# Block sums of batch 0's q and k: VectorE reductions in place of matmuls with a constant, with a new order of all steps

## The chip, the core and the metric

The kernel runs on one core of one Trainium2 chip. The core has five engines with a queue each: TensorE (PE) multiplies matrices into PSUM, VectorE (DVE) and ScalarE (ACT) work on PSUM and SBUF, GpSimd (POOL) works on SBUF alone, SyncE (SP) issues DMA transfers; GpSimd and ScalarE can issue them too. An engine takes the instructions of its queue in order and waits on semaphores for the others. The metric is the device time of one execution in microseconds (us); lower is better.

## The reference

The computation is an attention layer with two branches and a feed-forward layer behind it. Batch is 8, heads 8, sequence 576, head size 64.

```python
q_d = q.reshape(B, H, Sd, 4, D).mean(axis=3)      # the same for k_d and v_d
out_d = sm_attn(q_d, k_d, v_d)                    # full softmax attention over 144 means
out_up = np.repeat(out_d, 4, axis=2)
mask = np.abs(pos[:, None] - pos[None, :]) < 4
scores = np.where(mask, scale * q @ k.T, -1e9)    # scale = 1/8
out_local = softmax(scores) @ v
x = (out_up + out_local)                          # to (4608 tokens, 512)
h = x @ w_in                                      # 512 x 2048
g = np.where(h > 0, h, np.exp(np.minimum(h, 0)) - 1)
return g @ w_out                                  # 2048 x 512
```

The means of four consecutive rows of q and k are what the change is about: they are the "coarse" queries and keys.

## The kernel before

The work goes by batch and, within a batch, by pairs of heads (j = 0 to 3): two heads of 64 fill the 128 partitions. For each pair q and k are loaded with the tokens on the partitions, turned so that the head's dimension is on the partitions, and copied from PSUM to SBUF. The scores of near keys and of coarse keys go to PSUM, ScalarE takes the exponential, TensorE sums the denominators with indicator matrices, VectorE takes reciprocals, TensorE spreads these over the partitions, and a product of values and exponentials is scaled by them (the normalisation). Near and coarse parts are added into tiles of 512 tokens (`xt`). The feed-forward layer takes these tiles t = 0 to 8: 16 products with `WI` per tile (`h`), the activation by ScalarE and VectorE (`he`, `hg`), and for tiles 0 to 5 the products with `WO` (`y`), a copy (`yc`) and a store (`ys`). Tiles 6 to 8 go by a scheme of seven products of half-size blocks (`sm`, `p`, `pk`, `pf`, `ps`, with weight differences `wd`).

Batch 0 has code of its own, since everything waits for it. Its pairs 1 to 3 come by loads that cast to 16 bits on the way (`lc`, on GpSimd's queue, `load_cast`, L371); pair 0 comes in 32 bits on SP's queue (`lx`) and is cast by ScalarE and VectorE (`cx`, L405). `transposes` (L486, step `T`) turns q into the PSUM tile `tq` and k into `tk`; both come from the two-buffer tag `misc` (`one`, L302). For batch 0 it then forms the block sums on TensorE as well: twelve matmuls per tensor (six for pair 0) with the constant `R` write them into columns 736 to 1023 of the same PSUM tile (L507 to L523). Four evictions follow for each pair: `eq` and `ek` copy the turned q and k to `QT` and `KT` (L528, L535), `sq` and `sk` copy the sums to `qd` and `kd` (`first_sums`, L1140). `first_scores` (L1152, step `s.j.g`, for half g of the sequence) needs all four. `R` holds 0.25 at the right places (L163), so `qd` and `kd` are means.

For batches 1 to 7 the sums already come from the turned tensors: `sums` (L547) reduces on VectorE (`"k"`, `"Q"`) or in two additions on GpSimd (`"q"`).

The order of all work is written out by hand in the string `ORDER` (L41). Each word is a step, such as `eq.0.2` for the copy of q of batch 0 and pair 2; `at` (L1241) binds it to a function, and a word with `'` takes the other variant, mostly another engine (`on_dve`, `on_act`). Each engine's queue is its steps in the order of this string. Buffers with more than one copy take the copy that `SLOTS` (L231) lists. `Z` steps and the `fills` (L1273) are matmuls on zeros between the real ones.

The steps that the prediction follows are: `T`, `eq`, `ek`, `sq`, `sk`, `s`, `x` (exponentials), `fD`, `fdr`, `fP`, `fpc`, `fO`, `fN`, `fna` of batch 0 (denominators, reciprocals, spread, its copy, outputs, normalisation, addition); and for batch 1 `m` (mask, L666), `D` and `dr` (denominators L678, reciprocals L699), `P` (spread, L759), among the feed-forward steps `h`, `he`, `hg` of tile 0.

Of the kernel before, what the change touches and what calls it, by code (L numbers as in the profile page):

```python
# [41 lines left out]
cI empties cN lc.0.2.k lc.0.2.q cR lc.0.1.k lc.0.3.k lc.0.1.q lx.0.0.k zeros edges Z.1 T.0.2.(0,2) eq.0.2'  # L42
ek.0.2' sq.2.q' cx.0.0.k sk.2.k' s.2.1.2 T.0.1.(0,0) Z.0 s.2.0.2 cVR lv.0.3 cIND cv.0.3 lc.0.3.q lv.0.1
lx.0.0.q close lc.1.0.q eq.0.1' sq.1.q' ek.0.1' sk.1.k' cx.0.0.q T.0.0.(1,0) s.1.0.0 eq.0.0' sq.0.q' ek.0.0
sk.0.k' x.2.0 lc.1.2.q lc.1.1.q T.0.3.(0,0) lv.0.0 lv.0.2 wi.0 wi.2 x.1.0 wi.1 cv.0.0 lc.1.0.k s.0.0.1 cFOUR
eq.0.3' sk.3.k' ek.0.3' sq.3.q' wi.3 cSEL cv.0.2' cv.0.1' fV.3 s.3.0.1 x.0.0 fD.0.0 fdr.0 x.2.1 x.3.0 s.0.1.1
fV.1 fvc.1' x.0.1 cIND2 cVR2 cMASK s.3.1.0 lv.1.0 x.3.1 fD.1.0 Z.2 s.1.1.0 lv.1.1 lx.2.1.q fdr.1 x.1.1 fvc.3
fP.0.0 fV.0 fvc.0' fO.0.1 fV.2 fpc.0 fN.0 fvc.2 fD.2.0 fdr.2 fP.1.1 fD.3.0 fpc.1 fna.0.0 fO.1.4 fN.1 fna.1.0'
lx.2.1.k H.0 H.1 fP.2.0 lx.2.3.q lx.2.0.q fdr.3 fpc.2 fO.2.0 fN.2 H.2 fP.3.0 H.3 lc.1.3.q lc.1.3.k lc.1.1.k
h.0.0 h.0.1 he.0.0 he.0.1' fO.3.2 lc.1.2.k cv.1.0 fpc.3' fN.3 fna.3.0 lv.1.2 T.1.0 h.0.7 h.0.5 T.1.3 ek.1.0  # L50
eq.1.0 fna.2.0 sq.1.0 wo.0 he.0.5 hg.0.1' sk.1.0 lv.1.3 lx.2.2.k hg.0.0 hg.0.5 eq.1.3 ek.1.3 T.1.1 eq.1.1
h.0.6 ek.1.1' lx.2.0.k sk.1.1 he.0.6' he.0.7 hg.0.7 hg.0.6' sq.1.1 sq.1.3 cv.1.1 fna.2.1 cv.1.2 h.0.8 T.1.2
he.0.8 eq.1.2 ek.1.2 h.0.9 sk.1.3 sk.1.2 sq.1.2' hg.0.8 lv.2.0 s.1.1 sd.1.1 h.0.15 x.1.1.0 he.0.15 x.1.1.1
m.1.1 Z.4 h.0.10 Z.3 he.0.10 hg.0.10 s.1.3 sd.1.3 x.1.3.0 x.1.3.1 hg.0.15 h.0.2 s.1.2 sd.1.2 x.1.2.0 he.0.2'
he.0.9 x.1.2.1 wo.1 cv.1.3 cx.2.0.q wo.2 cx.2.0.k cv.2.0 cx.2.1.q cx.2.1.k lv.2.1 m.1.2 m.1.3 hg.0.9 s.1.0
sd.1.0 h.0.11 h.0.12 hg.0.2' x.1.0.0 lx.2.2.q m.1.0 V.1 x.1.0.1 he.0.11 h.0.3 he.0.3 vc.1 D.1 fna.3.1' dr.1
P.1.3 h.0.4 P.1.1 hg.0.11 pc.1.1' pc.1.3 hg.0.3 P.1.2 y.0.0 he.0.4' pc.1.2 on.1.1 of.1.1 T.2.0 y.0.4 wo.3
lv.2.2 n.1.1 on.1.3 of.1.3 ek.2.0 eq.2.0 n.1.3 hg.0.4' cv.2.1 y.0.5 y.0.1 P.1.0 on.1.2 of.1.2 pc.1.0 he.0.12'
a.1.1.2 a.1.1.1' cx.2.2.q cx.2.2.k a.1.3.2' n.1.2 a.1.2.1 lv.2.3 lx.2.3.k lx.3.0.k cv.2.2 cx.2.3.q cx.2.3.k
cv.2.3' cx.3.0.k y.0.6 h.0.14 y.0.2 on.1.0 of.1.0 sk.2.0 a.1.3.1' hg.0.12' sq.2.0 n.1.0 a.1.0.1' y.0.7 T.2.1  # L60
eq.2.1 sq.2.1 y.0.3 yc.0.0 he.0.14 ek.2.1 yc.0.1' T.2.2 ek.2.2' hg.0.14 sk.2.2 h.1.0 h.0.13 he.1.0 eq.2.2
he.0.13' hg.1.0 sk.2.1 hg.0.13' T.2.3 h.1.1 lx.3.2.q lv.3.0 lx.3.1.k lx.3.1.q lx.3.0.q lv.3.1 lx.3.2.k s.2.0
sd.2.0 eq.2.3 a.1.2.2 sq.2.3 y.0.12 h.1.5 he.1.1' hg.1.1' ek.2.3 he.1.5' x.2.0.0 hg.1.5' y.0.8 h.1.7 he.1.7'
s.2.1 sd.2.1 x.2.0.1 x.2.1.0 x.2.1.1 m.2.0 sk.2.3 hg.1.7' sq.2.2' y.0.13 y.0.14 h.1.3 y.0.9 s.2.2 sd.2.2
he.1.3 fl.3.0 ys.0.1 ys.0.0 lv.3.2 lx.3.3.k hg.1.3 cx.3.0.q cv.3.0 T.3.0 cx.3.1.k cx.3.1.q cv.3.1 cx.3.2.k
# [1360 lines left out]
```

## Time and profile before

| what | value |
|---|---|
| timed runs | 346.63, 347.79, 340.81 us (median 346.63) |
| the profiled execution's own time | 340.41 us |
| its span, first to last instruction | 338.6 us |
| mean granted TensorE clock | 0.99 |
| DMA | 50.09 MB, mean 148 GB/s |

The page gives the busy time of each engine over the span, the span in 40 slices of 8.5 us, and the groups of instructions. In the views, "x12" counts instructions, the arrow is "out<-in", and a bracket holds the idle time of the engine ahead of an instruction with what ended it. TensorE's durations are modelled with their drain, so that neighbours overlap; start-to-start distances say how long a group holds the engine. Stage views have columns of busy us and counts per engine, then the granted clock, the DMA share and GB/s. Group views give count, busy us, mean ns of one, and the idle time before them.

### The profile page before, as it was taken

To read this page: it belongs to the slowest core of one execution; us is meant where nothing else is said; L and a number is where in the kernel's file an instruction comes from. 1 tells how busy PE (TensorE), PEld (TensorE's weight loads), DVE (VectorE), ACT (ScalarE), POOL (GpSimd) and SP (SyncE) were. 2 spreads that over 40 slices of the span, in tenths; PEclk is the share of its full clock that TensorE was granted. 3 is DMA by queue.
4 is the path that set the end of the run, shared out by engine and by line. 5 is a ranking of instruction groups with operands and counts; after the bars stand their busy time and mean duration, and the time that the engine had idled before them with its cause. 6 is when DMAs were issued, how large, how long until landed. Compare 5 with 4: busy or idle time off the path is not lost.

```text
span 338.6 us, 10715 instructions
## 1 busy us (share of the span) xinstructions
PE 326.5 (96%) x4378; PEld 195.1 (58%) x4378; DVE 246.0 (73%) x481; ACT 215.2 (64%) x375; POOL 176.3 (52%) x283
## 2 busy tenths in 40 slices
PE   7999987999999999999999999999999999999996
PEld 2666875564554545554545454545445566766785
DVE  1455986697878777777778868777885879697663
ACT  2084886368788785655678748665766578666520
POOL 4374746498186446553263347578301793550380
PEclk9999997899999999999999999999999999999999
DMA  8999999999999989979999999776015000030043
GB/s 171 224 173 208 247 221 223 210 202 163 183 198 156 190 207 197 199 163 161 200 201 203 173 200 164 174 160 113 2 37 151 5 0 0 2 149 9 0 157 124
DMA packets 111314, 50.09 MB, mean 148 GB/s; under 512 B 95697, under 2 KB 105761, under 8 KB 111265
## 3 DMA queue, kind: packets, MB, share of 16 engines
q1 hardware_dynamic: 106961, 43.04, 66.5%
q0 software_dynamic: 4064, 6.26, 10.6%
q8 instruction: 34, 0.56, 0.7%
q10 hardware_dynamic: 240, 0.11, 0.1%
q14 instruction: 15, 0.12, 0.1%
HBM read 41.97 MB, written 9.55 MB: 152 GB/s over the span
## 4 chain that ended last, share of the span: by engine, by line
PE 75%; DVE 9%; DMA 6%; ACT 4%; issue 3%; SPq 2%; POOL 0%; DVEq 0%; ACTq 0%; POOLq 0%
PE hp L904 28%; PE op L945 21%; PE y L1017 6%; PE xz L1017 5%; DMA q<-in_q_dram 4%; DMA out_dram<-os 3%; PE hp L880 2%; PE lg L784 2%; PE tqk L502 2%; DVE gt L935 1%; PE sc L632 1%; DVE e L934 1%; DVE ke L550 1%; ACT r L925 1%; PE den L692 1%
## 5 line engine op out<-in xcount | busy, mean ns | idle before, releaser
L904 PE MATMUL hp<-xt,WI 128*128 128x512 f16 x512 | 128.6, 380 | 1.3 <-DVE gt L930 0.7
L945 PE MATMUL op<-WO,gt 128*128 128x512 f16 x384 | 96.4, 383 | 0.1
L904 PEld LDWEIGHTS <-WI 128*128 128x128 f16 x512 | 55.7, 114 | 44.4 <-issue 1.7
L930 DVE SCALAR_TENSOR_TENSOR gt<-e,hp 128x512 f16<-128x512 f16 x78 | 53.0, 683 | 30.6 <-ACT e L926 30.3
L925 ACT ACTIVATE r<-hp 128x512 f32<-128x512 f32 x78 | 46.7, 599 | 38.3 <-PE hp L904 30.5
L945 PEld LDWEIGHTS <-gt 128*128 128x128 f16 x384 | 35.8, 98 | 40.5 <-issue 1.4
L915 ACT ACTIVATE e<-hp 128x512 f16<-128x512 f32 x66 | 39.3, 597 | 25.0 <-PE hp L904 18.8
L926 ACT ACTIVATE e<-r 128x512 f16<-128x512 f32 x78 | 49.2, 631 | 2.5
L935 DVE SCALAR_TENSOR_TENSOR gt<-hp,e 128x512 f16<-128x512 f32 x66 | 45.7, 692 | 2.6
L868 POOL TENSOR_TENSOR xt<-ln 128x192 f16<-128x192 f16 (+7 forms) x36 | 25.0, 706 | 33.8 <-DVE ln L857 30.3
L655 ACT ACTIVATE pex<-sc 128x580 f16<-128x580 f32 (+1 forms) x56 | 31.1, 591 | 4.0 <-PE sc L645 3.9
L934 DVE TENSOR_SCALAR e<-e 128x512 f16<-128x512 f16 x66 | 24.2, 366 | 12.5 <-ACT e L915 12.1
L476 POOL CAST v<-v 128x640 f16<-128x640 f32 (+1 forms) x19 | 14.4, 759 | 25.1 <-DMA v<-in_v_dram 21.9
L414 POOL CAST k<-k 96x768 f16<-96x768 f32 x24 | 20.3, 846 | 11.1 <-DMA k<-in_k_dram 11.1
L414 POOL CAST q<-q 96x768 f16<-96x768 f32 x24 | 19.7, 821 | 6.9 <-DMA q<-in_q_dram 6.8
L568 POOL TENSOR_TENSOR t<-qt 128x288 f32<-128x288 f16 x22 | 14.7, 668 | 16.2 <-ACT qt L532 11.9
L1017 PEld LDWEIGHTS <-gt 128*128 128x128 f16 x192 | 18.8, 98 | 5.6
L550 DVE TENSOR_REDUCE ke<-kt 128x145 f16<-128x580 f16 x28 | 21.0, 751 | 1.2 <-DMA kt<-k 1.1
L857 DVE TENSOR_TENSOR ln<-lg,rcb 128x580 f16<-128x580 f32 x28 | 21.0, 751 | 0.0
L995 POOL TENSOR_TENSOR s<-s,gt 128x512 f16<-128x512 f16 x8 | 9.8, 1224 | 19.3 <-DVE s L995 19.2
L880 PE MATMUL hp<-xt,WI 128*128 128x256 f16 x128 | 17.2, 283 | 1.3 <-DVE gt L935 1.2
L995 POOL TENSOR_TENSOR s<-gt 128x512 f16<-128x512 f16 x6 | 6.9, 1152 | 20.5 <-DVE gt L935 19.3
(148 smaller groups left out, 479.7 us busy)
## 6 DMA issues: line engine op xcount, KB each, us to landing
v<-in_v_dram SPq DMA_DIRECT2D x111, 80.0 KB, 4.2
k<-in_k_dram SPq DMA_DIRECT2D x25, 288.0 KB, 5.6
q<-in_q_dram SPq DMA_DIRECT2D x25, 288.0 KB, 6.5
out_dram<-os SPq DMA_DIRECT2D x24, 256.0 KB, 3.7
rcb<-rd SPq DMA_DIRECT2D x10, 364.0 KB, 5.6
out_dram<-ou SPq DMA_DIRECT2D x11, 256.0 KB, 2.2
WI<-in_moe_w_in_dram POOLq DMA_DIRECT2D x4, 512.0 KB, 9.5
WO<-in_moe_w_out_dram POOLq DMA_DIRECT2D x4, 512.0 KB, 7.4
```

The source lines that it names most:

```text
L414: nc.gpsimd.tensor_copy(out=x[:], in_=src)
L655: nc.scalar.activation(out=s["p"][:, :, a : a + n], in_=g2(sc, a, n), func=AF.Exp, scale=SCALE / 16 if a else SCALE,)
L868: (eng or nc.gpsimd).tensor_tensor(out=xt(t)[:, j, t0 - TBLK * t : t1 - TBLK * t], in0=ln[:, a:z], in1=_rep4(ln[:, ga : ga + (z - a) // 4] ...
L904: nc.tensor.matmul(hp, w_in(dc, fc), xts[t][:, dc, :], start=(dc == 0), stop=(dc == DMC - 1),)
L915: nc.scalar.activation(out=e, in_=hp, func=AF.Exp)
L925: nc.scalar.activation(out=r, in_=hp, func=AF.Relu, scale=-1.0)
L926: nc.scalar.activation(out=e, in_=r, func=AF.Exp, scale=-1.0)
L930: nc.vector.scalar_tensor_tensor(out=to, in0=e, scalar=-1.0, op0=AB.add, in1=hp, op1=AB.max)
L934: nc.vector.tensor_scalar(out=e, in0=e, scalar1=1.0, scalar2=-1.0, op0=AB.min, op1=AB.add)
L935: nc.vector.scalar_tensor_tensor(out=to, in0=hp, scalar=0.0, op0=AB.max, in1=e, op1=AB.add)
L945: nc.tensor.matmul(op_[:], gts[t][:, fc, 128 * tt : 128 * tt + 128], WO[:, fc, :], start=(fc == 0), stop=(fc == FCN - 1),)
L1017: nc.tensor.matmul(to, w, x, start=(k == 0 and n in (1, 2)), stop=(k == FH - 1), skip_group_check=n > 2,)
```

## The change

`transposes` no longer forms sums, the constant `R` and its load `cR` go, and `first_sums` reduces the copies `QT` and `KT` on VectorE. `sums(0, j, "Q")` is the reduction over four neighbours that later batches use; q's sums are then multiplied by 1/16 in place (a quarter for each of the two means), k's stay plain sums. `sq` and `sk` of batch 0 thus have no variant on ScalarE any more and come after `eq` and `ek` of their pair.

```diff
@@ transposes
-        if b == 0:
-            for t in (s["tq"], s["tk"]):
-                x = xs.pop(0)
-                for c in range(TPP):
-                    sums_of_4 = C["R"][:, SD * (c // 2) : SD * (c // 2) + SD]
-                    if j == 0:
-                        nc.tensor.matmul(
-                            t[:, 736:1024].bitcast(FP32), x[:, c, :, :].rearrange("p e d -> p (e d)"),
-                            sums_of_4, start=(c == 0), stop=(c == TPP - 1),
-                        )
-                        continue
...
@@ first_sums
-    def first_sums(j, x, copy=None):
-        s, copy = st[(0, j)], copy or act
+    def first_sums(j, x):
         if x == "q":
...
-            copy(out=s["qd"], in_=s["tq"][:, 736:1024].bitcast(FP32))
+            sums(0, j, "Q")
+            qd = st[(0, j)]["qd"]
+            nc.vector.tensor_scalar(out=qd, in0=qd, scalar1=0.0625, scalar2=None, op0=AB.mult)
             return
-        copy(
+        nc.vector.tensor_reduce(
             out=coarse_keys(0, j),
-            in_=s["tk"][:, 736:1024].bitcast(FP32).rearrange("p (c u) -> p c u", u=CG),
+            in_=KT[j][:, KO : KO + S].rearrange("p (c u f) -> p c u f", f=4, u=CG),
+            axis=AX.X, op=AB.add,
         )
```

`ORDER` and `SLOTS` are replaced as a whole: the same steps, without `cR`, in another order, many in another variant. The first lines of the order, before and after:

```diff
-cI empties cN lc.0.2.k lc.0.2.q cR lc.0.1.k lc.0.3.k lc.0.1.q lx.0.0.k zeros edges Z.1 T.0.2.(0,2) eq.0.2'
-ek.0.2' sq.2.q' cx.0.0.k sk.2.k' s.2.1.2 T.0.1.(0,0) Z.0 s.2.0.2 cVR lv.0.3 cIND cv.0.3 lc.0.3.q lv.0.1
+lc.0.2.q lx.0.0.q cVR lx.0.0.k lc.0.2.k empties zeros cI T.0.2.(0,2) ek.0.2 eq.0.2 sq.2.q sk.2.k edges
+lc.0.1.k Z.3 lc.0.1.q T.0.1.(0,0) cN cIND cVR2 lv.0.1 lc.0.3.k lc.0.3.q s.2.1.2 close ek.0.1 cx.0.0.k eq.0.1
...
```

Around batch 1's denominators (`D.1`), before and after:

```diff
-sd.1.0 h.0.11 h.0.12 hg.0.2' x.1.0.0 lx.2.2.q m.1.0 V.1 x.1.0.1 he.0.11 h.0.3 he.0.3 vc.1 D.1 fna.3.1' dr.1
-P.1.3 h.0.4 P.1.1 hg.0.11 pc.1.1' pc.1.3 hg.0.3 P.1.2 y.0.0 he.0.4' pc.1.2 on.1.1 of.1.1 T.2.0 y.0.4 wo.3
+hg.0.10 m.1.1 hg.0.9 s.1.2 sd.1.2 x.1.2.0 he.0.8' x.1.2.1 m.1.2 hg.0.8' h.0.4 Z.4 h.0.3 he.0.3 D.1 h.0.11 dr.1
+P.1.1 P.1.3 he.0.4 hg.0.4 pc.1.3' hg.0.3 pc.1.1 cv.1.3 V.1 h.0.12 vc.1 he.0.11 hg.0.11 on.1.3 on.1.1 of.1.3
...
```

Counted over the whole order: of batch 0's eight copies `eq` and `ek`, two run on VectorE (seven before); the four block-sum casts `fvc` all run on VectorE (two before); 73 of 144 activations take the form `he`/`hg` with one ScalarE pass and two VectorE passes (66 before); 16 of 32 casts of v run on ScalarE (13 before); one pair more of batches 3 to 7 is turned by TensorE instead of by a DMA (25 steps `T` without the mark, 24 before).

More of the change, by code (lines that the diff above doesn't have):

```diff
@@ L231 @@
 SLOTS = {
-    "end.hx": "0110101010101010",
-    "end.y": "010101",
+    "end.hx": "0101010101101101",
+    "end.y": "011010",
     "late.hp": (
-        "011010100010101010101001010100101010101010101010101010101101010101010101010101010101010101"
+        "010101100100101010101001010101010101010101101010101010101010101010101010101010101010010101"
         "010101010101010101010101010100101"
     ),
-    "lo.k32": "0120012012012010210210201",
-    "lo.q32": "0120010220121001201210210",
+    "lo.k32": "0120120210201201202102120",
@@ L259 @@
+    "sb.p": "0123456789ab42065317a9b842063517b98a",
+    "sb.qd": "01230123103213023102130231032130",
     "sb.rcb": "01010101",
-    "sb.v16": "01234567132057643120756403217456",
+    "sb.v16": "01234567103275640132756402314756",
     "sb.vdb": "0101010",
     "sb.xt": "012012012",
-    "tu.k16": "01230132013201320132012310321032",
-    "tu.pex": "0101010101010101010101",
-    "tu.q16": "01230102320132013201230130213031",
+    "tu.k16": "01230132103210321023012310231023",
+    "tu.pex": "0101010101010101010",
@@ L266 @@
+    "tu.q16": "01230132013201320132013210231031",
 }
@@ L505, in transposes @@
                 )
-        if b == 0:
-            for t in (s["tq"], s["tk"]):
-                x = xs.pop(0)
-                for c in range(TPP):
-                    sums_of_4 = C["R"][:, SD * (c // 2) : SD * (c // 2) + SD]
-                    if j == 0:
-                        nc.tensor.matmul(
-                            t[:, 736:1024].bitcast(FP32), x[:, c, :, :].rearrange("p e d -> p (e d)"),
-                            sums_of_4, start=(c == 0), stop=(c == TPP - 1),
-                        )
-                        continue
-                    for e in range(2):
-                        nc.tensor.matmul(
-                            t[64 * e : 64 * e + 64, 736:1024].bitcast(FP32),
-                            by_head(x)[:, e, D * c : D * c + D], sums_of_4,
-                            start=(c == 0), stop=(c == TPP - 1),
-                        )
     def in_order(t, to):
@@ L1283 @@
             at("lc", load_cast, 1, j, x)
-            at("sq" if x == "q" else "sk", first_sums, j, x, other=on_dve(first_sums))
+            at("sq" if x == "q" else "sk", first_sums, j, x)
         at("T", transposes, 0, j, fills["T"][j])
```

230 lines of the change are left out of this document (113 added, 117 removed).

## The prediction

> **What bounds the kernel now.** I read four views, in this order: the page's head and its 40 slices, the busy time by stage, the first 20 us in order of time, and the waits of TensorE.
>
> ```profile
> span 338.6 us, 10715 instructions
> PE 326.5 (96%) x4378; PEld 195.1 (58%) x4378; DVE 246.0 (73%) x481; ACT 215.2 (64%) x375; POOL 176.3 (52%) x283
> PEclk9999997899999999999999999999999999999999
> ```
> ```profile
> core 0: us, PE busy (x) PEld busy (x) DVE busy (x) ACT busy (x) POOL busy (x), PEclk, DMA share, GB/s
> 10.00:30.00 20.00, 18.18 (x419) 13.01 (x414) 11.02 (x27) 10.97 (x16) 8.57 (x14) 1.00 1.11 200
> 30.00:60.00 30.00, 26.95 (x526) 21.24 (x524) 23.84 (x47) 20.84 (x37) 19.90 (x37) 0.93 1.18 225
> 60.00:320.00 260.00, 258.46 (x3254) 144.33 (x3254) 201.01 (x371) 178.57 (x314) 133.52 (x216) 1.00 0.73 135
> 320.00:338.60 18.60, 15.28 (x137) 13.14 (x134) 8.71 (x17) 2.99 (x7) 9.63 (x9) 1.00 0.35 128
> ```
>
> TensorE is the bound: from 60 to 320 us it idles 260 − 258.46 = 1.5 us. Whatever ends sooner ahead of 60 us therefore moves the whole rest forward, one for one. The edit lies between 8 and 21 us, in the stage where TensorE is busy too (18.18 of 20 us), but in short pieces that hang on evictions; VectorE has 9 us free there. Between 30 and 60 us VectorE, ScalarE and TensorE limit each other, and the clock row dips: that is the one place where TensorE loses speed.
>
> ```profile
> 8.61 0.45 PE L497 MATMUL tq<-ID,q 96*64 96x96 f16 x12 [0.23 <-DMA q<-in_q_dram]
> 8.83 0.82 POOL L476 CAST v<-v 112x768 f16<-112x768 f32 x1 [4.19 <-DMA v<-in_v_dram]
> 9.60 1.25 POOL L373 DMA_DIRECT2D q<-in_q_dram  x2
> 9.81 0.54 PE L519 MATMUL tq<-R,q 96*64 96x144 f16 x12
> 10.19 0.54 PE L519 MATMUL tk<-R,k 96*64 96x144 f16 x12
> 10.40 0.76 DVE L532 COPY qt<-tq 128x576 f16<-128x576 f16 x1 [8.14 <-PE tq L519]
> 11.07 0.75 DVE L539 COPY kt<-tk 128x576 f16<-128x576 f16 x1
> 12.22 0.30 DVE L1147 CAST kd<-tk 128x144 f16<-128x144 f32 x1
> 12.57 0.29 PE L611 MATMUL sc<-qd,kd 64*112 64x72 f16 x4 [0.34 <-DVE kd L1147]
> 12.79 0.45 PE L497 MATMUL tq<-ID,q 96*64 96x96 f16 x12
> 17.05 0.54 PE L513 MATMUL tk<-R,k 96*128 96x144 f16 x6
> 18.37 0.45 PE L497 MATMUL tq<-ID,q 96*64 96x96 f16 x12 [0.16 <-DVE qd L1145]
> 31.38 0.91 DVE L835 TENSOR_TENSOR ln<-lg,rcb 128x720 f16<-128x720 f32 x1 [1.44 <-PE lg L823]
> 35.78 0.91 DVE L835 TENSOR_TENSOR ln<-lg,rcb 128x720 f16<-128x720 f32 x1 [0.53 <-PE lg L823]
> ```
>
> Here the reader sees one pair: transposes, sums on TensorE, four evictions on VectorE one behind the other, then the score. The next pair's transposes (12.79) come only when both PSUM buffers are read out.
>
> **The change, part by part.**
>
> *Sums off TensorE.* The rows at 9.81 and 10.19 start 0.38 us apart: twelve of these matmuls hold TensorE for 0.38 us. There are 36 + 36 + 6 + 6 = 84 in eight groups (the six at 17.05 are full-width and take as long), so 8 × 0.38 = 3.0 us of issue go.
>
> ```profile
> L519 PE MATMUL tq<-R,q 96*64 96x144 f16 x36 | 1.7, 226 | 0.0
> L513 PE MATMUL tk<-R,k 96*128 96x144 f16 x6 | 0.5, 226 | 0.0
> L1145 DVE CAST qd<-tq 128x144 f16<-128x144 f32 x4 | 1.2, 297 | 0.0
> L562 DVE TENSOR_REDUCE qd<-qt 128x144 f16<-128x576 f16 x1 | 0.7, 743 | 0.0
> L934 DVE TENSOR_SCALAR e<-e 128x512 f16<-128x512 f16 x9 | 3.4, 383 | 0.8 <-ACT e L915 0.8
> L388 DVE MEMSET q<- 1x1 f32 x3 | 0.2, 59 | 0.0
> L539 ACT COPY kt<-tqk 128x576 f16<-128x576 f16 x3 | 1.9, 643 | 0.0
> ```
>
> *Sums onto VectorE.* Eight reductions of 0.74 (the qd row is the very same shape) are 5.9 us; eight casts of 0.30 go, −2.4. Four multiplications of 128x144 in place have no row: at least 0.06 (a one-element memset), at most 0.38 (the 128x512 multiplication). I take 0.15, nearer the small end since 144 is a quarter of 512: 0.6 in all, bounds 0.2 to 1.5. Net +4.1 us of VectorE. A sentence on a page: the Trainium skill (VectorE: DVE Perf Modes, "The perf-mode tier table") gives a reduction one element per cycle and a 16-bit tensor_scalar up to four, which would put my multiplication at its lower end and change the sum by 0.3 us of VectorE at most.
>
> *Copies moved to ScalarE.* Before, seven of the eight first copies of tq and tk are VectorE's; after, two are. Five × 0.75 = −3.8 on VectorE, +5 × 0.64 = 3.2 on ScalarE. Two casts of v leave ScalarE for GpSimd, and the block-sum casts of v go to VectorE. VectorE ends within about 1 us of its load in this stage, ScalarE within 1 to 2 us. Both are about half idle from 10 to 30 us, so I cost the load itself at nothing; were that cover gone, it would cost up to the 4.1 us.
>
> *The chain of one pair.* What is not hidden is order: a sum now waits for its copy. For pair 2: transposes end at 9.98 in both, ScalarE's two copies end 1.15 later (0.5 apart and 0.64), and 0.7 + 0.1 + 0.7 of VectorE make 12.7, where 12.53 stood before. The first score is 0.15 us late. But the PSUM buffers are read out at 11.1, not 12.5, and the new order puts pair 1's transposes ahead of that score, so pair 1 starts 1.2 to 1.5 us sooner. The last score of each pair then waits for its k reduction, about 0.7 us behind the copy, under other pairs' transposes and scores. Following both orders pair by pair to the normalisation that feeds the first expert matmuls (31.38), I get 30.4: −1.0 us. Ends: −3.0, if all TensorE issue that goes was on the path, and +1.5, if two reductions in a row (1.5 us) hold the scores. I take −1.0, because the path goes through evictions more often than through TensorE.
>
> *Queues.* On GpSimd six loads of q and k are now issued one behind the other; before, the cast of v at 8.83, which waited 4.19 us for its data, stood ahead of pair 3's q load at 9.60. So pair 3 can be turned ahead of 18.37; that is in the walk. SP sends pair 0's q and k first and the mask constant behind them, about 1.5 us later than before and still about 8 us ahead of the first score. The constant's own load on ScalarE's queue goes: nothing, since ScalarE first waits for data anyway.
>
> *30 to 56 us, reordered.*
>
> ```profile
> PE den L692 <- DVE pex L670: 0.9, 1, 0.9
> PE rb L763 <- DVE rc L702: 0.8, 1, 0.8
> PE hp L880 <- DVE gt L935: 1.2, 3, 0.6
> ACT r L925 <- DMA out_dram<-os: 6.3, 3, 4.4
> ```
> ```profile
> 49.00:52.40 3.40, 3.17 (x54) 2.89 (x54) 2.56 (x8) 3.37 (x8) 2.33 (x5) 1.00 1.09 215
> 52.40:55.80 3.40, 1.66 (x69) 1.36 (x68) 2.76 (x5) 1.66 (x4) 1.24 (x3) 0.99 1.14 226
> 55.80:59.20 3.40, 3.40 (x26) 2.08 (x26) 1.15 (x3) 2.30 (x4) 3.03 (x7) 0.50 1.09 227
> 59.20:62.40 3.20, 3.20 (x44) 1.83 (x43) 1.90 (x5) 0.47 (x2) 1.42 (x4) 0.50 1.25 175
> ```
>
> TensorE waits 0.9 for the last mask, then 0.8 for the reciprocals, with nothing between; and 1.2 for gates. In the new order fewer gates stand ahead of the last mask, and one expert tile of about 0.95 us (four slots of 0.24) stands between denominators and their spread, which covers the 0.8. I take −1.0 of these 2.9 us, with ends −2.9 and +2.0 (VectorE gets three batch-1 sums or copies more here, 0.7 each).
>
> *The clock.* Half clock from 55.8 to 62.4 costs 6.6 × 0.5 = 3.3 us. It follows a stretch in which TensorE was busy 1.66 of 3.40 us. The same denominators, reciprocals and spreads still come one after another, so I leave the dip in: 0; ends −3.3 and +3.3.
>
> *The rest.* All later steps move, loads and stores on SP and casts on GpSimd among them. One more pair of a later batch is turned by TensorE instead of by a DMA (six transposes, 0.3 us). Seven more gates take the form with one ScalarE pass and two VectorE passes; beside a full TensorE that is nothing, as VectorE runs 201 of 260 us. I take +0.3, with −1.5 (all idle) and +4.4 (the longest wait on an output store, ScalarE's, should it come uncovered).
>
> **Sum.** The profiled execution took 340.41 us, 1.8 more than its span. 340.4 − 1.0 − 1.0 + 0 + 0.3 = 338.7, say 339. The three timed runs took 340.81, 346.63 and 347.79: the profiled one is like the lowest, and the median stands 6.2 us above it. No row of this trace says why, so a median of the changed kernel may stand as far above the sum, at 345.
>
> **Rivals.** *The dip goes.* For it: one wait covered, less VectorE ahead of the masks. Against it: the stage stays a chain of short matmuls. 338.7 − 3.3 = 335.4.
>
> *Nothing gained.* The sums' chain, copy, reduce, multiply, takes the place of the matmuls; for it the first score, which comes no sooner; against it the earlier PSUM release. The −1.0 in front falls away, as may that behind it: 340 to 341.
>
> *Slower: the clock drops in the front as well.* The 3.0 us taken out between 10 and 30 us leave TensorE with 15.2 of 20 us; where two reductions hold the scores, a stretch of 3.4 us can fall to the half that preceded 55.8. One more such dip costs 3.3: 342; two, or one that lasts twice as long, 345. It decides where such a stretch falls below about 1.7 of 3.4 us. Against it: the front as a whole stays near three quarters, and the filling matmuls stay. The Trainium skill has a rule that speaks for this rival (TensorE: Matmul & The Clock Gate, Part 1 and Part 4): a free-running window of about 3.4 us decides, and transposes do not count as busy in the same way, so real matmuls removed from among transposes leave less that counts. The 0.50 behind 52.4 to 55.8 agrees with the first half of it; of the second half no run here shows anything.
>
> *It doesn't do what it says.* The matmuls plainly go; that the reductions run on VectorE is in the diff. I give this no chance of its own.
>
> **How the numbers follow.** Forecast (336.5 to 341.5 by the profiled execution) 0.50; the dip goes 0.20 (333 to 336.5); nothing gained 0.15; slower 0.15 (342 to 347). The range from 333 to 347 takes in the first two, most of the others, and a median that stands above its lowest run by 6 us. 2% is 6.8 us here, about what a measurement of this kernel can tell from no change. Faster by more: only with the dip gone and much of the 3.0 in front, or where 339 is held against a run like 346.63; 0.22. Slower by more needs two dips or the 4.4 us on top of one: 0.08. Within: 0.70.
>
> **What would show it.** Right: no matmul on the constant; eight reductions of about 0.74 us before 25 us; pair 1's transposes about 1.3 us sooner; the normalisation of 31.38 at 30 to 31; the wait for the reciprocals near nothing. Wrong: the normalisation later than 31.4, a second stretch at 0.50 in the clock row, or TensorE idle above 1.5 us from 60 to 320 us.

## The result and the profile after

| | kernel before | changed kernel |
|---|---|---|
| median of the runs of the comparison (17 each) | 343.27 us (340.81 to 349.51) | 340.60 us (338.67 to 343.25) |
| ratio, 95% interval | 1 | 0.9944 (0.9918 to 0.9969) |
| profiled execution, its span | 340.41, 338.6 us | 340.32, 338.4 us |
| TensorE busy in that span | 326.5 us | 323.8 us |

The change makes the kernel 0.6% faster. The three runs that were shown with the kernel before (median 346.63) stood high: over the 155 runs of it that stand beside the comparisons of this study the median is 342.79, the lowest 337.94, the highest 351.61, and only nine reach 346.6. The ratios given with each run leave executions disturbed by more than 1.5% over the kernel's lowest out, and since the kernel before spreads without a gap, a ratio moves with its lowest run (337.94 to 340.81, by comparison); the medians of all runs therefore stand beside it. Taken over all 29 runs of the changed kernel and all 155 of the one before, the means are 340.82 and 342.80: 2.0 us, a ratio of 0.9942, 0.9923 to 0.9962 when the runs are resampled.

The head and the clock row of the page of the changed kernel, and its stages:

```profile
span 338.4 us, 10553 instructions
PE 323.8 (96%) x4300; PEld 191.9 (57%) x4300; DVE 250.0 (74%) x497; ACT 214.2 (63%) x373; POOL 165.6 (49%) x266
PEclk9999789999999999999999999999999999999999
```
```profile
10.00:30.00 20.00, 17.27 (x359) 11.88 (x360) 13.85 (x40) 11.61 (x17) 13.74 (x20) 1.00 1.09 197
30.00:60.00 30.00, 25.77 (x541) 20.05 (x539) 22.60 (x43) 20.15 (x36) 14.22 (x27) 0.89 1.18 210
60.00:320.00 260.00, 258.32 (x3235) 144.13 (x3228) 202.72 (x380) 176.60 (x313) 127.36 (x206) 1.00 0.69 136
```

TensorE has 2.7 us less to do, and the span is 0.2 us shorter: the rest came back as idle time, 12.1 us before (338.6 − 326.5) and 14.6 after. From 10 to 30 us it idles 2.73 instead of 1.82, from 30 to 60 us 4.23 instead of 3.05; from 60 to 320 us the two are alike (1.68 and 1.54).

The front of the changed kernel in order of time, VectorE and TensorE:

```profile
10.35 0.75 DVE L544 TENSOR_REDUCE qd<-qt 128x144 f16<-128x576 f16 x1 [8.22 <-ACT qt L514]
11.14 0.20 DVE L1126 TENSOR_SCALAR qd<-qd 128x144 f16<-128x144 f16 x1
11.25 0.74 DVE L1128 TENSOR_REDUCE kd<-kt 128x144 f16<-128x576 f16 x1
19.74 0.75 DVE L1128 TENSOR_REDUCE kd<-kt 128x144 f16<-128x576 f16 x1 [0.16 <-ACT kt L521]
28.53 0.91 DVE L817 TENSOR_TENSOR ln<-lg,rcb 128x720 f16<-128x720 f32 x1 [0.94 <-PE lg L805]
38.40 0.91 DVE L817 TENSOR_TENSOR ln<-lg,rcb 128x720 f16<-128x720 f32 x1 [1.25 <-PE lg L805]
```
```profile
8.65 0.45 PE L497 MATMUL tk<-ID,k 96*64 96x96 f16 x12
10.52 0.45 PE L497 MATMUL tq<-ID,q 96*64 96x96 f16 x12 [0.89 <-DMA q<-in_q_dram]
12.23 0.26 PE L593 MATMUL sc<-qd,kd 64*112 64x72 f16 x4
```

The reader sees the eight reductions (the first and the last on `kd` here) done by 20.5 us, pair 1's transposes at 10.52 (12.79 before), and the second normalisation at 28.53 (31.38 before). Pair 2's transposes of k, at 8.65, are sooner too (9.53 before), since its q is now the first load on GpSimd's queue. But the last normalisation comes at 38.40, where it came at 35.78. The lead of 2.85 us is spent behind 30 us, and the waits of TensorE up to 60 us say on what (the longest of the list, 2.1 us on the zeros at the start, stands in both kernels and is left out):

```profile
PE tqk L497 <- DMA q<-in_q_dram: 1.3, 1, 1.3
PE sc L627 <- POOL qd L552: 1.1, 1, 1.1
PE tq L497 <- DMA q<-in_q_dram: 0.9, 1, 0.9
```

The wait for the reciprocals is gone, as forecast. In its place TensorE waits 1.3 us for batch 1's first q and 1.1 us for a sum over q on GpSimd. That q is the first of two loads that GpSimd issues here; in the kernel before it was the second of the two at 9.60:

```profile
22.71 1.27 POOL L373 DMA_DIRECT2D q<-in_q_dram  x2
```

Each of the two waits is followed by half clock (stages of the changed kernel):

```profile
32.20:34.80 2.60, 1.31 (x59) 1.12 (x48) 1.32 (x3) 2.13 (x4) 0.00 (x0) 0.98 1.28 199
34.80:38.20 3.40, 3.40 (x38) 2.06 (x37) 2.35 (x5) 1.25 (x2) 2.35 (x4) 0.52 1.30 219
46.70:48.50 1.80, 0.67 (x30) 0.46 (x20) 1.70 (x3) 0.47 (x2) 1.16 (x3) 0.95 1.34 208
48.50:51.90 3.40, 3.40 (x36) 2.19 (x38) 3.15 (x8) 2.01 (x5) 0.00 (x0) 0.52 1.10 223
```

Busy 1.31 of 2.60 us, then 3.4 us at half clock; busy 0.67 of 1.80, then 3.4 us more. Together they are as long as the one stretch of the kernel before (6.8 us).

Where the 2.0 us between the means lie, the kept profiles don't show. The first product with `WO` comes at 58.51 us in the first profile of the kernel before and at 56.68 in its second (`before_again` below). In the changed kernel it comes at 60.26, and at 64.09 and 58.84 in two more profiles of the same program up to there (`after_again`, `half_stores`), with about half a us more work ahead of it. None of these leads by as much as 1 us at 60 us.

### The profile page after: what moved, and what is told of

Read it like the earlier page. It is cut to its first block, busy times and chain, and to the rows that moved or that the text cites. A ratio compares the mean times of both kernels' runs of the same rounds, so it can differ in the third digit from the quotient of the medians.

```text
span 338.4 us, 10553 instructions
## 1 busy us (share of the span) xinstructions
PE 323.8 (96%) x4300; PEld 191.9 (57%) x4300; DVE 250.0 (74%) x497; ACT 214.2 (63%) x373; POOL 165.6 (49%) x266
## 4 chain that ended last, share of the span: by engine, by line
PE 72%; DMA 13%; SPq 6%; POOL 4%; issue 2%; ACT 1%; DVE 1%; POOLq 0%; ACTq 0%
PE hp L886 29%; PE op L927 22%; PE y L999 6%; DMA v<-in_v_dram 5%; PE xz L999 5%; DMA MASK<-MASKc 5%; DMA q<-in_q_dram 3%; SPq L429 3%; PE hp L862 2%; PE lg L766 2%; SPq L451 2%; PE sc L614 1%; PE tqk L502 1%; POOL xt L850 1%; PE lg L786 1%
## 5 line engine op out<-in xcount | busy, mean ns | idle before, releaser
L927 PE MATMUL op<-WO,gt 128*128 128x512 f16 x384 | 94.3, 379 | 0.1
L912 DVE SCALAR_TENSOR_TENSOR gt<-e,hp 128x512 f16<-128x512 f16 x71 | 48.1, 683 | 27.3 <-ACT e L908 26.9
L897 ACT ACTIVATE e<-hp 128x512 f16<-128x512 f32 x73 | 43.5, 599 | 36.5 <-PE hp L886 29.5
L907 ACT ACTIVATE r<-hp 128x512 f32<-128x512 f32 x71 | 42.5, 598 | 32.5 <-PE hp L886 30.0
L917 DVE SCALAR_TENSOR_TENSOR gt<-hp,e 128x512 f16<-128x512 f32 x73 | 50.5, 692 | 2.9
L908 ACT ACTIVATE e<-r 128x512 f16<-128x512 f32 x71 | 44.8, 631 | 2.3
L916 DVE TENSOR_SCALAR e<-e 128x512 f16<-128x512 f16 x73 | 27.3, 374 | 21.1 <-ACT e L897 20.8
L850 POOL TENSOR_TENSOR xt<-ln 128x128 f16<-128x128 f16 (+7 forms) x37 | 26.1, 717 | 33.4 <-DVE ln L839 28.2
L476 POOL CAST v<-v 128x640 f16<-128x640 f32 (+1 forms) x16 | 12.2, 771 | 27.0 <-DMA v<-in_v_dram 21.2
L544 DVE TENSOR_REDUCE qd<-qt 128x144 f16<-128x576 f16 x13 | 9.6, 742 | 9.1 <-ACT qt L514 9.0
```

Of the source, the lines that this page charges most:

```text
L850: (eng or nc.gpsimd).tensor_tensor(out=xt(t)[:, j, t0 - TBLK * t : t1 - TBLK * t], in0=ln[:, a:z], in1=_rep4(ln[:, ga : ga + (z - a) // 4] ...
L897: nc.scalar.activation(out=e, in_=hp, func=AF.Exp)
L907: nc.scalar.activation(out=r, in_=hp, func=AF.Relu, scale=-1.0)
L908: nc.scalar.activation(out=e, in_=r, func=AF.Exp, scale=-1.0)
L912: nc.vector.scalar_tensor_tensor(out=to, in0=e, scalar=-1.0, op0=AB.add, in1=hp, op1=AB.max)
L916: nc.vector.tensor_scalar(out=e, in0=e, scalar1=1.0, scalar2=-1.0, op0=AB.min, op1=AB.add)
```

## The experiments

Four more comparisons of four kernels each, beside fresh runs of the kernel before. All of them are in the table; the median in brackets is that of the kernel before beside it. The clock is the mean over the runs of the mean granted clock; (1 − clock) × span is the time lost to it if TensorE is the bound.

| kernel | ratio, 95% interval | median us | mean clock |
|---|---|---|---|
| before_again | 1.0003 (0.9955 to 1.0051) | 342.56 (342.51) | 0.996 |
| sums_only | 1.0074 (1.0023 to 1.0126) | 343.81 (342.51) | 0.974 |
| order_only | 1.0024 (0.9987 to 1.0060) | 342.57 (342.51) | 0.996 |
| early_pair | 0.9991 (0.9957 to 1.0025) | 341.90 (342.51) | 0.981 |
| late_fill | 1.0063 (1.0030 to 1.0096) | 343.69 (342.14) | 0.991 |
| early_sum | 0.9934 (0.9893 to 0.9974) | 339.39 (342.14) | 0.990 |
| half_stores | 0.9972 (0.9939 to 1.0004) | 340.66 (342.14) | 0.991 |
| sums_copies | 1.0032 (0.9997 to 1.0068) | 343.01 (342.14) | 0.982 |
| after_again | 1.0000 (0.9952 to 1.0047) | 340.88 (343.18) | 0.988 |
| early_sum_again | 0.9979 (0.9935 to 1.0022) | 340.10 (343.18) | 0.995 |
| early_both | 0.9977 (0.9936 to 1.0017) | 340.53 (343.18) | 0.994 |
| sums_fill | 1.0004 (0.9965 to 1.0044) | 341.24 (343.18) | 0.995 |
| after_fill | 0.9958 (0.9928 to 0.9987) | 340.54 (342.91) | 0.996 |
| early_fill | 0.9961 (0.9927 to 0.9994) | 340.65 (342.91) | 0.996 |
| before_fill | 0.9990 (0.9950 to 1.0030) | 342.42 (342.91) | 0.993 |
| sums_fill_again | 0.9960 (0.9928 to 0.9993) | 342.07 (342.91) | 0.996 |

The kernel before itself has a mean clock of 0.9925 over the 138 runs for which it is known, the changed kernel 0.9897 over 29.

**Which part does what.** The kernel before again, the sums alone, and the order alone:

> The kernel before, unchanged, profiled once more. If the execution that the forecast was built on was an unusually fast one, a second profile shows a longer span, about 341.5 us (its median of 343.3 less 1.8), with more than the one stretch of 6.8 us at half clock, or with TensorE idle above 1.5 us from 60 to 320 us. If that execution was typical, the span is 338 to 339 again and the timed runs stand higher for another reason. The ratio is 1.000 either way.

> Only the sums go to VectorE; the order, buffers and engines are those of the kernel before (the copy of pair 3's k moves one place, ahead of its sum). Theory F (feed: the front's gain was real and was given back because batch 1's loads come later in the new order): loads are as before, so no wait for batch 1's q; all copies and sums on VectorE make about 4 us more of its work between 10 and 21 us, so the normalisation that stood at 31.38 us comes at 31 to 32.5; ratio to before 0.998 to 1.005. Theory V (the reductions themselves cost what the front gained): slower than before, ratio 1.005 to 1.01.

> The new order, buffers and engines, but the sums stay matmuls with the constant, and VectorE evicts them (six words of the order move up so that the PSUM buffers are read in time). Theory F: the normalisation (31.38 before, 28.53 after) at 29.5 to 31, since 3.0 us of TensorE come back but 4 us of VectorE go; the loads of batch 1 stay late, so the first transposes of batch 1 still start near 33.7 and the time is that of the changed kernel, ratio to before 0.994 to 1.000. Theory V: without the reductions it is faster than the changed kernel, ratio 0.985 to 0.991.

`sums_only` has the new `first_sums` in the order of before; `order_only` has the matmuls with `R` in the new order.

```diff
 sums_only: the order of before, without the constant
-cI empties cN lc.0.2.k lc.0.2.q cR lc.0.1.k
+cI empties cN lc.0.2.k lc.0.2.q lc.0.1.k
...
-eq.0.2' ek.0.2' sq.2.q' cx.0.0.k sk.2.k'
+eq.0.2' ek.0.2' sq.2.q cx.0.0.k sk.2.k
...
 order_only: the new order, with the constant
-empties zeros cI T.0.2.(0,2) ek.0.2 eq.0.2 sq.2.q sk.2.k
+empties zeros cI cR T.0.2.(0,2) ek.0.2 eq.0.2 sq.2.q' sk.2.k'
```

Neither half of the change gains by itself: the sums alone cost 0.7%, the order alone brings nothing (342.57 against 342.51), and both together are 0.6% faster. The front shows the same in profiles without half clock up to there. This is the second normalisation in the kernel before (`before_again`), with the order alone, with the sums alone (`sums_fill_again`, explained below) and with both (`half_stores`, the changed kernel up to 60 us):

```profile
31.34 0.91 DVE L835 TENSOR_TENSOR ln<-lg,rcb 128x720 f16<-128x720 f32 x1 [1.48 <-PE lg L823]
32.24 0.91 DVE L833 TENSOR_TENSOR ln<-lg,rcb 128x720 f16<-128x720 f32 x1 [0.84 <-PE lg L821]
32.63 0.91 DVE L815 TENSOR_TENSOR ln<-lg,rcb 128x720 f16<-128x720 f32 x1 [1.44 <-PE lg L803]
29.78 0.91 DVE L817 TENSOR_TENSOR ln<-lg,rcb 128x720 f16<-128x720 f32 x1 [0.94 <-PE lg L805]
```

Only both together bring it forward. `order_only` misses what was expected of it, 29.5 to 31 us.

**Why the sums alone lose.** TensorE's busy time and clock by stage in `sums_only`, and its waits from 10 to 18 us, in an execution of 350.22 us, the longest of the twelve:

```profile
10.00:18.00 8.00, 4.98 (x82) 3.35 (x80) 6.49 (x12) 1.03 (x2) 1.97 (x4) 1.00 1.15 215
18.00:35.00 17.00, 16.33 (x257) 10.37 (x254) 8.35 (x18) 10.32 (x15) 8.09 (x12) 0.51 1.01 191
```
```profile
PE tq L500 <- DVE q L410: 1.5, 1, 1.5
PE sc L591 <- DVE kd L1126: 1.5, 1, 1.5
```

From 10 to 18 us TensorE is busy 4.98 of 8.00 us (7.30 in the kernel before), since VectorE, at 6.49 of 8.00, holds both the copies and the reductions; then 17 us go by at half clock. This is the prediction's slower rival, in the front. It isn't one execution's alone: none of the twelve runs of `sums_only` had a full clock (0.965 to 0.990). Two remedies were tried, the copies on ScalarE, and zeros for TensorE to multiply while it waits:

> The kernel before with the sums of batch 0 on VectorE (1.0074 of the kernel before as it stands, in the order of before) and with the copies of the turned q and k of pairs 2, 1 and 3 moved from VectorE to ScalarE, no other word moved. The theory that the sums cost time in the old order because VectorE holds the copies as well, so that the first transposes and score products wait and TensorE's clock drops: the ratio falls to 1.000 or below and the first normalisation is back at 28.5 us or sooner. The rival, that the reductions cost what they cost wherever the copies are: it stays at 1.005 or above.

> The sums on VectorE in the order of before (sums_only, 1.0074 of the kernel before), with 12 matmuls on zeros (12 x 0.2157 = 2.6 us at full clock) ahead of the first score products of the four pairs, in place of the 40 small matmuls that the sums took from TensorE there. The theory that the price of sums_only is the clock that falls when TensorE waits in the front: the clock stays near full between 10 and 40 us and the ratio is 1.000 to 1.003. The rival, that the waits for VectorE themselves are the price: the fills lie within the waits or lengthen them, and the ratio stays at 1.006 to 1.012.

```diff
 sums_copies: the order, batch 0's copies of pairs 2, 1 and 3 on ScalarE
-eq.0.2' ek.0.2'
+eq.0.2 ek.0.2
...
-eq.0.1' sq.1.q ek.0.1'
+eq.0.1 sq.1.q ek.0.1
...
-eq.0.3' ek.0.3'
+eq.0.3 ek.0.3
 sums_fill: first_scores
-        keep(sc, n)
+        keep(sc, n + 3 * ((j, g) in ((2, 1), (1, 0), (0, 0), (3, 0))))
```

The copies on ScalarE raise the clock only to 0.982 and leave the ratio at 1.0032, between the two expectations: no decision. The zeros decide. They add 2.6 us of work to TensorE, and the same two stages read:

```profile
10.00:18.00 8.00, 5.56 (x75) 3.52 (x73) 6.46 (x13) 1.31 (x3) 1.46 (x3) 0.94 1.25 213
18.00:35.00 17.00, 16.50 (x336) 11.19 (x334) 10.40 (x23) 11.02 (x15) 10.08 (x16) 0.93 1.05 192
```

The clock from 18 to 35 us is 0.93 instead of 0.51, the mean clock of the runs 0.995 instead of 0.974, and the ratio 1.0004 and, in the repeat, 0.9960; the mean time of the 24 runs is 341.7 us where `sums_only` has 344.6 (2.9 us less, 1.4 to 4.7). More work in the front makes the kernel 2.9 us faster, because it keeps TensorE's clock.

> sums_fill once more (mean clock 0.9945 against 0.9743 of sums_only; median 341.2 against 343.2 of the kernel before beside it). If the sums on VectorE bring their 2.9 us of TensorE work only as far as the clock is held, in whichever order, the ratio is 0.994 to 1.000 and the mean clock 0.992 or more; if the last result was that chip's or that hour's, the clock falls to 0.98 and the ratio rises to 1.003 or more.

The repeat holds (clock 0.996). So the loss of the sums in the old order is that of a front in which TensorE starves. That the sums would pay in this order is not shown: with the zeros TensorE has about as much work as in the kernel before (3.0 us less, 2.6 more), and the 1.1 us (0.4 to 1.8) by which the 24 runs lie under the 155 are about what their higher clock is worth (0.995 against 0.9925, 0.85 us).

**Does a delay at 60 us reach the end?** The premise "one for one" was tested by adding work, and two parties that might take it up, the stores and the loads:

> The changed kernel with 14 matmuls on zeros put ahead of the first product of the output projection, at about 60 us: 14 x 0.2157 = 3.0 us more on TensorE, everything else as in the changed kernel (0.9944 of the kernel before). The prediction's premise was that TensorE carries every delay at 60 us one for one to the end: then the run ends 3.0 us later, a ratio to the kernel before of about 1.003. The rival: behind 60 us transfers (loads of the tiles ahead, stores of the output) set part of the pace and take up a delay as they wore off a lead; then the run ends 1 us later or less, a ratio of 0.995 to 0.998.

> The changed kernel with every second store of the first six tiles' output left out (12 of 24; those rows of the output are not written), the work on the engines unchanged. If the stores and the buffers behind them set part of the pace from 60 to 210 us, the run ends 1 to 3 us sooner than the changed kernel: ratio to the kernel before 0.986 to 0.991. If TensorE alone sets it, or the loads do, no change: 0.994 plus or minus 0.003.

```diff
 late_fill: mm2
             ops[(t, tt)] = bank("misc", "op")
+            if (t, i) == (0, 0):
+                keep(ops[(t, tt)], 14)
 half_stores: store
+        if tt % 2:
+            return
```
```profile
60.37 3.19 PE L1046 MATMUL op<-Z 128*128 128x512 f16 x14
63.40 2.75 PE L929 MATMUL op<-WO,gt 128*128 128x512 f16 x12
```

The fill moves the first products of `WO` by 3.0 us, and the mean of all runs by 2.8 (2.1 to 3.4) against the changed kernel's 29. One for one, for a delay. A lead isn't always kept: the first product with `WO` is 1.9 us sooner than the changed kernel's in the profile of `early_sum` (58.37 against 60.26), and its span is 2.0 us shorter; in that of `early_both` it is 1.3 us sooner (58.98), and the span is 1.6 us longer. Half the stores left out change nothing (340.66 against 340.60; the means differ by −0.2, −1.0 to +0.6), so the 1 to 3 us that stores setting the pace would cost aren't there. In the order of before it is less clean: in the profile of `before_again`, set beside the first one instruction by instruction, TensorE is 2.08 us ahead at 60 us and 0.28 at the end; part of that lead was lost at turned keys (`ke`) that a transfer brought late. That is one pair of executions, and nothing more was tried on it.

**What eats the lead behind 30 us.** Three edits of the order: batch 1's first loads ahead of the weights, GpSimd's sum ahead of the cast it stood behind, and that with a gentler move of the loads:

> The changed kernel with one thing moved: the loads of batch 1's pair 0 (k and q) are issued ahead of the first two weight loads on GpSimd's queue, at about 16.4 us in place of 22.1 and 22.7. Theory F: TensorE's wait of 1.29 us for that q at 33.7 goes, and with it the stretch at half clock that follows it (1.7 us); 1.5 to 3 us less, ratio to before 0.985 to 0.990, if nothing later takes it back. Rival T (transfers as a whole bound the stage from 10 to 50 us, whatever their order): the wait turns up elsewhere, at the weights or at batch 1's v, and the ratio stays 0.993 to 0.997. Theory V: no change, 0.994.

> The changed kernel with GpSimd's sum over q of batch 1's pair 3 put ahead of the cast of v's third tile, so that it no longer stands behind the landing of that tile at 44 us. The theory that this one wait at 48.0 us (1.13 us of TensorE) comes from the order on GpSimd: the wait and the stretch of half clock behind it go, the multiplications of batch 1 are 1 to 2 us sooner, and of that a third to all is left at the end: ratio to the kernel before 0.988 to 0.993. The rival, that the transfers as a whole bound this stage: the wait comes back at the next operand (the sum of v or the cast for pair 3's scores), and the ratio stays at 0.994 plus or minus 0.003.

> The changed kernel with the one sum over q ahead of the cast of v, once more (0.9934, 0.9893 to 0.9974, and in the profile 2.0 us shorter than the changed kernel). If the lead of 1.7 us that the profile showed at 48 us is carried to the end, the ratio is 0.988 to 0.992; if it was that one execution's, it is 0.994 like the changed kernel's.

> early_sum with the loads of q and k of batch 1's pair 0 also issued 2 us sooner on GpSimd's queue: ahead of the spread of the selection constant and of the last block of weights, but not ahead of the casts of v that early_pair delayed. If the order on that queue sets when q lands (34.2 us in early_sum, issued at 22.8), TensorE's waits for it at 33 us (0.9 and 0.5 us) go and the run ends about 1 us before early_sum: ratio 0.986 to 0.991. If the transfers as a whole set it, q lands no sooner or something else is later in its place: the same as early_sum.

```diff
 early_pair
-wi.1 wi.2 lc.1.1.k wi.0 cv.0.3 lv.0.2 cv.0.2 cSEL wi.3 lc.1.0.k lc.1.0.q
+lc.1.0.k lc.1.0.q wi.1 wi.2 lc.1.1.k wi.0 cv.0.3 lv.0.2 cv.0.2 cSEL wi.3
 early_sum
-cv.1.1' fna.3.0 cv.1.2 sq.1.2 wo.0 h.0.15 h.0.8 s.1.1 lv.2.0 hg.0.2 he.0.15 hg.0.15 sk.1.2 sd.1.1 x.1.0.1
-hg.0.7' x.1.1.0 sq.1.3 fna.2.1'
+cv.1.1' fna.3.0 sq.1.3 cv.1.2 sq.1.2 wo.0 h.0.15 h.0.8 s.1.1 lv.2.0 hg.0.2 he.0.15 hg.0.15 sk.1.2 sd.1.1 x.1.0.1
+hg.0.7' x.1.1.0 fna.2.1'
 early_both: early_sum, and
-cSEL wi.3 lc.1.0.k lc.1.0.q
+lc.1.0.k lc.1.0.q cSEL wi.3
```

Loading q sooner buys nothing: the mean of `early_pair` is 1.2 us (0.4 to 1.9) over the changed kernel's. In its profile TensorE meets a longer wait elsewhere, on the cast of v that now stands behind two more issues on GpSimd's queue:

```profile
PE vs L566 <- POOL v L474: 2.3, 1, 2.3
```

`early_both` avoids that, and its wait for q is gone between 30 and 60 us. In its place stands one for the last block of weights, which was moved back:

```profile
PE hp L860 <- DMA WI<-in_moe_w_in_dram: 1.3, 1, 1.3
```

Its median is no better than `early_sum`'s. This fits the rival that the transfers as a whole bound this stage (210 GB/s from 30 to 60 us, 136 behind it) and their order only chooses which one is late; two orders argue for it and don't show it. Moving the sum does what it should. In GpSimd's queue of the changed kernel and then of `early_sum`:

```profile
44.15 0.72 POOL L476 CAST v<-v 128x640 f16<-128x640 f32 x1 [3.80 <-DMA v<-in_v_dram]
46.78 0.68 POOL L550 TENSOR_TENSOR t<-qt 128x288 f32<-128x288 f16 x1
47.53 0.43 POOL L552 TENSOR_TENSOR qd<-t 128x144 f16<-128x144 f32 x1
```
```profile
40.69 0.67 POOL L548 TENSOR_TENSOR t<-qt 128x288 f32<-128x288 f16 x1 [0.99 <-ACT qt L512]
41.43 0.42 POOL L550 TENSOR_TENSOR qd<-t 128x144 f16<-128x144 f32 x1
44.28 0.72 POOL L474 CAST v<-v 128x640 f16<-128x640 f32 x1 [2.42 <-DMA v<-in_v_dram]
```

The cast stands 3.80 us for v, and the sums behind it with it: the one that TensorE waits for is done at 47.96. Put ahead, it is done at 41.85, and the wait of 1.1 us is gone. The mean of 22 runs is 340.09, 0.7 us under the changed kernel's, with an interval from −1.5 to +0.1: faster than the kernel before (0.9921 over all runs, 0.9901 to 0.9942), and not told apart from the changed kernel. The repeat's ratio of 0.9979 misses its expectation, the ratio of its medians (0.991) doesn't. It has the lowest time seen here.

**Does the clock explain the rest?** Two executions of the changed kernel can differ by more than the change brings:

> The changed kernel once more, beside the kernel before on the same chip. If the first comparison (0.9944, 0.9918 to 0.9969) is sound, the ratio falls at 0.992 to 0.997. Which TensorE clock stretches the profile shows is not expected to repeat: two other programs that are the same up to 60 us showed none.

The repeat has the same median, 340.88, and the ratio of the medians is 0.993; the ratio of 1.0000 lies outside what was expected, since that comparison has one of the lowest runs of the kernel before (337.96). Its profiled execution took 344.99 us, with a span of 343.1, and one view of it shows the difference of 4.7 us to the first:

```profile
10.00:22.00 12.00, 9.57 (x135) 6.30 (x135) 9.11 (x23) 6.41 (x11) 6.97 (x11) 0.86 1.00 188
22.00:36.00 14.00, 13.51 (x230) 8.61 (x231) 6.64 (x18) 5.75 (x7) 6.65 (x10) 0.63 1.16 206
```

Half clock for most of 22 to 36 us, the second normalisation at 34.59 instead of 28.53. `late_fill` and `half_stores`, which are the changed kernel up to 60 us, had no half clock at all, with waits of 1.8 and 2.0 us at the same sum. The same program draws anything from none to some 17 us of it (three stretches of 3.4, 10.2 and 3.4 us in this execution). Over 138 runs of the kernel before, those with a mean clock below 0.9865 average 344.9 us, those from 0.9935 up 341.6; of the changed kernel 342.4 and 340.1. In each class, and in the one between them, the changed kernel is ahead, by 1.5 to 2.8 us, so its gain isn't one of clock.

Three kernels put zeros into the waits ahead of such stretches:

> The changed kernel with 5 matmuls on zeros (5 x 0.2157 = 1.1 us) ahead of the first scores of pair 0, where TensorE waited 0.4 to 1.3 us at about 21 us, and 16 small transposes of zeros (about 0.8 us) ahead of batch 1's first transposes, where it waited 0.9 to 1.3 us for q at about 33 us. If the waits are what lets the clock drop, the runs' mean clock rises from 0.988 (the changed kernel's last twelve runs) to 0.994 or more, and the median falls from 340.7 by 1 to 2 us: ratio to the kernel before 0.987 to 0.991. If not, the clock stays and the fills cost up to their own 1.9 us: 0.995 to 1.000.

> early_sum (340.1 and 339.4 in the two calls) with the same two fills. If the waits let the clock drop: mean clock 0.995 or more and a median of 338 to 339, ratio 0.986 to 0.990. If not: 340 to 342, ratio 0.993 to 0.999.

> The kernel before with 4 matmuls on zeros (0.9 us) ahead of batch 1's denominators and 3 (0.6 us) ahead of its first spread, where its TensorE waited 0.91 and 0.84 us ahead of its own half-clock stretch at 56 us: the prediction's rival that the dip goes, by itself. If those waits cause it, the mean clock (0.9925 over 103 runs) rises to 0.996 or more and the median falls by 1 to 2 us: ratio 0.994 to 0.997. If the stretch comes from elsewhere or only moves, 1.000 to 1.004.

```diff
 after_fill, early_fill: first_scores, transposes
-        keep(sc, n)
+        keep(sc, n + 5 * ((j, g) == (0, 0)))
-            keep(t, n)
+            keep(t, n + 4 * ((b, j, name) == (1, 0, "tq")))
 before_fill: denominators, spread
+        keep(den, 4 * (b == 1))
+        keep(rb, 3 * ((b, j) == (1, 3)))
```

In the changed kernel the clock rises as expected, from 0.990 to 0.996, and the time stays (340.54): the clock that is won is about what the zeros cost. `early_fill` is the same case (340.65, no better than `early_sum`). In the kernel before the zeros do neither: clock 0.993, time as before; its stretch isn't cured there. What the waits do to the clock is shown by `sums_only` with and without zeros; that the dips behind 30 us are worth curing is not.

## Why the prediction was right or wrong

- **The number, 339.0 us: 1.6 us under the changed kernel's median, and against the median that stood beside it, 346.63, a gain of 2.2% where 0.6% was measured.** The step that failed is the base of the sum: "340.4 − 1.0 − 1.0 + 0 + 0.3 = 338.7, say 339", made against one execution that lies 2.4 us under the median of 155 (22 of these 155 are as low or lower), and held against a median of three that lies 3.8 us over it. The terms themselves add up to −1.7 us, and −2.0 (−2.6 to −1.3) was measured; on a base of 342.8 they give 341.1, where the changed kernel's medians are 340.6 and 340.9. That they come so near is luck in part: the two terms of −1.0 were wrong in opposite directions, as shown below. The text saw the gap ("a median of the changed kernel may stand as far above the sum, at 345") but kept the low base for its number.
- **"No row of this trace says why" the median stands higher: this stays open.** The clock spreads the runs, but it isn't what made the base low: that execution had a clock of 0.990, under the mean of 0.9925, and `before_again` has a median of 342.56 at a mean clock of 0.996. Waits behind 60 us differ from one execution to the next as well: the second profile lost 1.8 us there that the first didn't. No profile of the kernel before near its median was kept.
- **"TensorE is the bound ... one for one": right** in the changed kernel for a delay (2.8 us at the end for 3.0 put in at 60 us); a lead at 60 us was kept in the profile of `early_sum` and lost in those of `early_both` and `before_again`.
- **Sums off TensorE, 3.0 us: right as work** (busy time −2.7), **not as time**: idle time grew by 2.5 in the profile.
- **The front, −1.0 with ends −3.0 and +1.5: under-sized where the clock holds.** The normalisation forecast at 30.4 came at 28.53, and at 29.78 and 30.08 in `half_stores` and `late_fill`, the same program up to there: a lead of 1.3 to 2.85 us. Where the clock drops ahead of it, it comes as late as 34.59, beyond the end of +1.5. Pair 1's transposes came 2.27 sooner, not 1.2 to 1.5. The walk has pair 2's "transposes end at 9.98 in both"; its k is turned 0.88 sooner, since its q is loaded first. What ended pair 1's wait was its own q's landing (0.89 us), no longer PSUM. The reductions (0.74 to 0.75) and multiplications (0.20, taken as 0.15) were right, or nearly.
- **30 to 56 us, −1.0 with ends −2.9 and +2.0: wrong in sign.** The wait for the reciprocals went, but the whole lead did too: batch 1's denominators start at 54.91 (53.72 before), at 53.50 in `half_stores` and 55.03 in `late_fill`, where no half clock disturbs; 53.04 in `before_again`. The named end "VectorE gets three batch-1 sums or copies more" wasn't it; the waits are for transfers and for a GpSimd sum behind a cast that waits for one. The queue was looked at for the front ("six loads ... one behind the other") and not for this stage.
- **The clock left in at 0: right for the profiled pair** (6.8 us of half clock in both), in two pieces. Over the runs the loss is about 3.5 us (0.0103 × 340) after and 2.6 before.
- **"The rest", +0.3:** TensorE's idle time from 60 to 320 us is 1.68 and 1.54; nothing to tell from zero.
- **The slower rival, the clock drops in the front: its mechanism is real.** It is what the sums do in the old order (ratio 1.0074), and what some executions of the changed kernel show; its price of 3.3 us a dip is too low for `sums_only`, where one stretch lasts 17 us, and its condition of about 1.7 of 3.4 us is too strict: 1.93 of the 3.4 us ahead of that stretch were busy. The rule cited there from the Trainium skill (TensorE: Matmul & The Clock Gate, Part 1) of a free-running window of about 3.4 us agrees: the stretches in these traces are 3.41 us or multiples of it, and where they fall differs from run to run. That transposes count for less (the same page of the Trainium skill, Part 4) was not separated from the lack of work as such.
- **The signs.** The matmuls on the constant are gone, the eight reductions end by 20.5 us and the wait for the reciprocals went. Two signs of being wrong came too: a second stretch at half clock, and TensorE idle for more than 1.5 us from 60 to 320 us (1.68, though the kernel before had 1.54).
- **The chances:** within 2% had 0.70, and the range of 333 to 347 holds the time. That 340.6 lies in the forecast's own band of 336.5 to 341.5 is luck: a base 2.4 us too low. It lies as well at "340 to 341", the price of the rival "nothing gained".

## What to carry to other kernels

Make the sum against the same statistic that it will be held against: one profiled execution of a kernel whose clock varies can lie 1% off the median, and its clock alone doesn't say which way (0.990 in the low one here, 0.9925 over the runs). Work taken off the bounding engine in a start-up stage cost time here where nothing filled its place; a few matmuls on zeros in `sums_only` were worth 2.9 us, while in the changed kernel, which starves less, they only paid for themselves. A cast that waits for a load holds up everything behind it on its queue: put the operand that the bounding engine needs next ahead of it.

## What the hardware showed that was not expected

- TensorE fell to half clock though no single wait of it ahead of the drop was longer than 1.5 us: busy 1.31 of 2.60 us was enough ahead of 34.8 us, and 4.98 of 8.00 with waits of 1.5 and 1.5 us ahead of 18 us; once down, it stayed down for 17 us in `sums_only` although it was busy 16.33 of 17.00 us.
- The same does not drop it every time: with a wait of 2.0 us at the same place `half_stores` kept the full clock. The same program's mean clock ran from 0.974 to 0.998 (the changed kernel again), and its runs from 339.2 to 345.0 us, the longest at the lowest clock.
- Within a trace the stretches at half clock start on a grid of 3.41 us. On this grid the step ahead of a drop had TensorE busy for 1.1 to 2.5 of its 3.41 us, but steps with 1.8 to 1.9 also passed without one (`half_stores`, `early_both`, `order_only`). So no busy share that decides it is shown.
